# Windowed attention and a gated network on one core: w_out sums moved out of the first pair, a classic second down projection, and activation splits on VectorE

## The chip, the core and the metric

The kernel runs as one program on 1 core of one Trainium2 chip. The metric is the device time of that core in microseconds (us). The core has a matrix engine (TensorE, PE in the profile, with its weight loads as PEld), three engines for elementwise work (VectorE or DVE, ScalarE or ACT, GpSimd or POOL) and SyncE (SP), whose queue starts all the transfers. Each engine works through its own instruction list in order, and waits on semaphores where an operand or a buffer isn't ready.

## The reference

Everything is float32 at the edges; the weights reach the program as 64-bit patterns, which it converts itself. Cut to what matters:

```python
# q, k, v: 8 x 8 x 576 x 64;  w_gate, w_val: 512 x 1536;  w_out: 1536 x 512
scores = 1/sqrt(64) * q @ k^T
scores = where(0 <= i - j < 64, scores, -1e9)        # causal window of 64
attn   = exp(scores - max);  attn = attn / (sum(attn) + 1e-9)
x      = (attn @ v) as 4608 tokens x 512
out    = (sigmoid(x @ w_gate) * (x @ w_val)) @ w_out
```

## The kernel before

**Tiles and pairs.** The 4608 tokens are 12 tiles of 384, worked on as six pairs, which I call pair 0 to pair 5. In each pair a stage of *ups* (x times w_gate and w_val, sigmoid and product: 1536 hidden features for 768 tokens) comes before a stage of *downs* (hidden times w_out). Between these matmuls stand those of the attention that makes x for the next pair. It is cut into eight *units* a pair, each a tile and a quarter of the features. A unit is scores (L219) and softmax minima on VectorE (L243) with exponentials on ScalarE (L251), then the normalization by a factor (L268), on GpSimd but for one quarter, then transposes on TensorE (`pp`, L299) with their copies `pT` on ScalarE (L304), and last the products with v (`oo`, L328), copied out as `xf` by ScalarE (L282, L316).

**Exactness.** A float32 operand is split into a rounded high part and a low rest, and each block product takes three matmuls: high by high, high by low, low by high (`three`, L583). So an activation block needs a *part* before TensorE can use it: a ScalarE copy for the high half (L671), a subtraction for the low half (L673).

**Pair 0** is classic: `up` (L358), sigmoid (L367), gate times value (L386), `down`. Meanwhile the 36 weight blocks (12 each of w_gate, w_val and w_out) arrive as integers and are converted, two ScalarE activations (`conv_a`), three VectorE bit operations (`conv_b`, L126 to L130) and a split (`conv_c`, L158) each. Converted float32 blocks of w_gate and w_val are stored to the scratch arrays `w32d` (L98). As soon as two blocks of w_out are there, `wo_sums` (L462) forms their sums on GpSimd in pieces of 128 columns, and stores them to `wod`.

**Pairs 1 to 5** save matmuls by a Strassen-Winograd scheme: seven block products instead of eight, from four weight sums (S1 to S4) and activation differences (T1 to T4); the table is `PRODUCTS`. The ups of a pair are 84 products of six matmuls (`product`, L612), as six blocks k of seven products n. The downs are 42 parts (seven products of six blocks k), each against two outputs with three matmuls, 252 in all (`last_product`, L676). The differences of x are made by `x_prep` and `x_part` (L562 to L577), those of the hidden blocks by `h_prep` and `h_part` (L661 to L674); `h_engine` and `x_engine` put them on VectorE in pair 1 (but for the last k) and on GpSimd from pair 2 on. `h_part` makes its low half on GpSimd for products 2 and 6. In the ups of pair 1 the gate and value sums are made from `w32d` as well (`sums_load`, `sums_make`, `sums_split`, `sums_store`).

**Order.** TensorE's instructions keep the order of the program. That order comes from due times written by hand: `put(time, order, function, ...)` collects events, the list is sorted, and the functions are called in turn. `visit(("u", i) ...)` and `visit(("d", i) ...)` attach an attention stage of a unit behind up product i or down part i. A scheduler places the instructions of the other engines; a buffer that comes from a pool by its tag (`raw`, `w32`, `W`, `x0` to `x13`, `wo_0` to `wo_6`) makes its new user wait for the last reader of the old one. TensorE's output banks are `b0` and `b1` with three buffers each: ups and downs share them, so a down's first matmul waits for VectorE's last reads of an up's bank (`c` at L625, `h` at L629).

The listing below gives the functions that the change touches, with the lines of the profile.

Of the kernel before, what the change touches and what calls it, by code (L numbers as in the profile page):

```python
# [18 lines left out]
P = 128  # L19
BLK = 64  # L20
TT = 384
# [5 lines left out]
def attn_ffn(ctx: ExitStack, tc: tile.TileContext, qT, kT, vN, w_gate, w_val, w_out, out, outT):  # L27
# [70 lines left out]
    w32d = [[dr.tile([P, DM], F32, name=f"w32d_{m}_{j}") for j in range(NF)] for m in range(2)]  # L98
# [33 lines left out]
    def conv_c(i):  # L132
# [15 lines left out]
        else:  # L148
            cp = split(w32.rearrange("p (a h) -> p a h", a=2), w2[:, :, 0, :], w2[:, :, 1, :], nc.vector)
            wgv[m][j] = w2  # L150
            nc.sync.dma_start(out=w32d[m][J], in_=w32)
            for name, half in (("A11", 0), ("A12", 1)) if J < NK else (("A22", 1),):
                put_part(m, J % NK, name, w2[:, half])
        marks[("w", i)] = (cp,)
# [241 lines left out]
    def get_hidden(t, j):  # L396
        hb = mp.tile([P, 2, TT], F32R, name=f"hb_{t}_{j}", tag="raw", bufs=RAW)
# [63 lines left out]

    def wo_sums(k):  # L462


        cols = [slice(c, c + P) for c in range(0, H, P)]
        b = [xp.tile([P, 3, H], F32, name=f"b{i}_{k}", tag=f"x{12 + i}") for i in range(2)]
        for i in range(2):
            src = wo_all[2 * k + i].bitcast(F32).rearrange("p e (a h) -> p e a h", a=2)
            for a in range(2):
                for c in cols:  # L470
                    nc.gpsimd.tensor_add(out=b[i][:, a, c], in0=src[:, 0, a, c], in1=src[:, 1, a, c])
        for c in cols:
            nc.gpsimd.tensor_add(out=b[0][:, 2, c], in0=b[0][:, 1, c], in1=b[1][:, 1, c])
        for c in cols:
            nc.gpsimd.tensor_sub(out=b[1][:, 2, c], in0=b[0][:, 2, c], in1=b[0][:, 0, c])
        for c in cols:
            nc.gpsimd.tensor_sub(out=b[0][:, 1, c], in0=b[0][:, 0, c], in1=b[0][:, 1, c])
        for c in cols:
            nc.gpsimd.tensor_sub(out=b[1][:, 0, c], in0=b[1][:, 0, c], in1=b[1][:, 2, c])
        for i, (names, at) in enumerate(((("S3", "S1"), (1, 2)), (("S4", "S2"), (0, 2)))):  # L480
            hi = xp.tile([P, 2, H], F32R, name=f"bh{i}_{k}", tag=f"x{10 + i}")
            for e, (name, a) in enumerate(zip(names, at)):
                for c in cols:
                    nc.gpsimd.tensor_copy(out=hi[:, e, c], in_=b[i][:, a, c])
                for c in cols:
                    nc.gpsimd.tensor_sub(out=b[i][:, a, c], in0=b[i][:, a, c], in1=hi[:, e, c].bitcast(F32))
# [461 lines left out]
```

## Time and profile before

| quantity | value |
|---|---|
| median of 3 runs | 1011.53 us |
| lowest and highest | 1008.22 and 1012.38 us |
| the profiled execution, its time | 1010.89 us |
| its span | 1009.1 us |
| mean granted TensorE clock | 0.991 |
| DMA | 275.04 MB, 273 GB/s mean |
| end of pair 0 | 231.6 us from the start of the span |

The span is the time from the first to the last instruction that the profiler saw. The page gives the busy time of each engine, which is an average over stages with different limits: pair 0 has conversions and no Strassen scheme, pair 5 has no attention beside it. So the profile is to be read stage by stage. In a row of groups, "out<-in" gives the operation's result and operands by the names in the program, x the count, and the last part the idle time of the engine ahead of them with the instruction that ended it.

### The profile page before, as it was taken

How to read it: one execution, taken by the hardware profiler on the slowest of the kernel's cores; microseconds unless marked ns; L12 is line 12 of the kernel's file. 1: busy time of each engine (PE TensorE's matmuls, PEld its weight loads, DVE VectorE, ACT ScalarE, POOL GpSimd, SP SyncE). 2: the span in 40 equal slices, each digit the busy share in tenths (PEclk: the TensorE clock that was granted, in tenths of full speed). 3: DMA queues.
4: the chain of work that ended last, by engine and by line, in shares of the span. 5: the costliest groups of instructions: out<-in, count | busy, mean ns of one | idle time of the engine just before them, and what ended most of it. 6: DMA issues, size and time to landing. Idle time of an engine off the chain costs nothing.

```text
span 1009.1 us, 20697 instructions
## 1 busy us (share of the span) xinstructions
PE 956.9 (95%) x7164; PEld 904.2 (90%) x7164; DVE 686.3 (68%) x1681; ACT 588.5 (58%) x1469; POOL 482.3 (48%) x626
## 2 busy tenths in 40 slices
PE   6997998999999899999989999989999989999998
PEld 5886997879998899999889999979999979999988
DVE  7899998856777867555766455776555675655762
ACT  7876776637667565555665555575545666412341
POOL 4269759977673742131755113565122474111552
PEclk9999999999999999999999999999999999999999
DMA  9899998999897689888769888768978865888454
GB/s 347 304 352 337 367 332 293 325 344 328 318 322 257 234 256 313 268 263 263 249 193 307 273 271 262 251 212 280 299 259 263 260 218 190 300 261 248 130 191 164
DMA packets 109832, 275.04 MB, mean 273 GB/s; under 512 B 11936, under 2 KB 42784, under 8 KB 109728
## 3 DMA queue, kind: packets, MB, share of 16 engines
q1 hardware_dynamic: 109728, 273.73, 81.5%
q8 instruction: 57, 0.93, 0.4%
q14 instruction: 47, 0.39, 0.1%
HBM read 220.99 MB, written 52.69 MB: 271 GB/s over the span
## 4 chain that ended last, share of the span: by engine, by line
PE 63%; DVE 18%; ACT 8%; DMA 4%; POOL 3%; issue 3%; SPq 0%; DVEq 0%; POOLq 0%; ACTq 0%
PE pr L586 35%; PE y L586 17%; DVE h L673 7%; PE ph L358 3%; ACT p L251 2%; PE s L219 2%; PE pp L299 2%; PE y L411 2%; DVE h L629 2%; DVE w L130 1%; PE s L328 1%; POOL h L673 1%; DVE w L128 1%; DVE w L158 1%; ACT h L671 1%
## 5 line engine op out<-in xcount | busy, mean ns | idle before, releaser
L586 PE MATMUL y<-h,wot 128*128 128x384 f32 x1260 | 231.0, 341 | 15.3 <-DVE h L673 5.9
L586 PEld LDWEIGHTS y<-h,wot 128*128 128x128 f32 x1260 | 222.1, 191 | 19.8 <-DVE h L673 7.2
L586 PE MATMUL pr<-x_T,wt 128*128 128x384 f32 x1224 | 226.1, 336 | 1.4 <-DVE c L596 1.2
L586 PEld LDWEIGHTS pr<-x_T,wt 128*128 128x128 f32 x1224 | 211.8, 188 | 3.4 <-DVE c L596 2.3
L586 PE MATMUL pr<-x_B,wt 128*128 128x384 f32 x1008 | 187.4, 336 | 0.0
L586 PEld LDWEIGHTS pr<-x_B,wt 128*128 128x128 f32 x1008 | 175.0, 188 | 3.2 <-issue 3.1
L268 POOL TENSOR_TENSOR p<-p,rs 128x384 f32<-128x384 f32 x76 | 68.9, 921 | 207.1 <-DVE rs L259 191.6
L671 ACT CAST h<-h 128x384 fp32r<-128x384 f32 x210 | 100.9, 513 | 79.3 <-PE y L586 39.6
L673 DVE TENSOR_TENSOR h<-h,h 128x384 fp32r<-128x384 f32 x150 | 115.6, 803 | 41.8 <-ACT h L671 41.7
L367 ACT ACTIVATE g<-c 128x384 f32<-128x384 f32 x90 | 47.3, 525 | 141.2 <-DVE c L625 141.0
L251 ACT ACTIVATE p<-p,mn 128x128 f32<-128x128 f32 x288 | 111.1, 393 | 24.6 <-DVE mn L243 24.2
L358 PE MATMUL ph<-x,w 128*128 128x384 f32 x576 | 108.7, 343 | 4.1 <-ACT g L367 2.9
L358 PEld LDWEIGHTS ph<-x,w 128*128 128x128 f32 x576 | 101.5, 191 | 7.2 <-ACT g L367 3.6
L629 DVE TENSOR_TENSOR h<-c,g 128x384 f32<-128x384 f32 x90 | 64.5, 716 | 39.2 <-ACT g L367 33.3
L673 POOL TENSOR_TENSOR h<-h,h 128x384 fp32r<-128x384 f32 x60 | 64.7, 1088 | 53.8 <-ACT h L671 52.9
L243 DVE CUSTOM_DVE_ANT_0 p<-s,m 128x128 f32<-128x128 f32 x288 | 65.4, 283 | 19.8 <-PE s L219 19.8
L596 DVE TENSOR_TENSOR c<-pr,p 128x384 f32<-128x384 f32 x60 | 33.1, 551 | 55.1 <-PE pr L586 55.1
L304 ACT COPY pT<-pp 128x384 f32<-128x384 f32 x96 | 41.3, 480 | 37.7 <-PE pp L299 37.7
L219 PE MATMUL s<-k,q 64*64 64x128 f32 x1152 | 47.5, 292 | 11.6 <-ACT xf L316 5.5
L549 POOL TENSOR_TENSOR h<-h 128x384 f32<-128x384 f32 x21 | 23.7, 1128 | 65.7 <-DVE h L629 65.7
L299 PE MATMUL pp<-ident,p 128*128 128x128 f32 x288 | 43.9, 282 | 9.6 <-POOL p L268 6.8
L219 PEld LDWEIGHTS s<-k,q 64*64 64x64 f32 x1152 | 34.4, 140 | 18.6 <-ACT xf L316 6.4
(114 smaller groups left out, 1500.5 us busy)
## 6 DMA issues: line engine op xcount, KB each, us to landing
wt<-wd SPq DMA_DIRECT2D x186, 512.0 KB, 4.4
wot<-wod SPq DMA_DIRECT2D x105, 512.0 KB, 4.4
v<-in_vN_dram SPq DMA_DIRECT2D x48, 384.0 KB, 5.2
wd<-ws SPq DMA_DIRECT2D x48, 256.0 KB, 5.3
k<-in_kT_dram SPq DMA_DIRECT2D x48, 224.0 KB, 4.8
q<-in_qT_dram SPq DMA_DIRECT2D x48, 192.0 KB, 4.6
wd<-w SPq DMA_DIRECT2D x36, 256.0 KB, 5.1
out_dram<-yo SPq DMA_DIRECT2D x39, 192.0 KB, 4.6
```

Of the source, the lines that this page charges most:

```text
L219: pe(nc.tensor.matmul(sc[h][half * BLK:(half + 1) * BLK, u, :], qt[h * BLK:(h + 1) * BLK, U * BLK:(U + 1) * BLK], kt[h * BLK:(h + 1) * BLK ...
L243: nc.vector.tensor_tensor_reduce(out=pt[:, u, :], in0=sc[:, u, :], in1=masks[key], op0=ALU.add, op1=ALU.min, scale=-SCALE, scalar=3.0e38, ...
L251: exp = nc.scalar.activation(pt[:, u, :], pt[:, u, :], AF.Exp, bias=mn[:, u:u + 1], scale=-1.0, **sums)
L268: eng.tensor_mul(out=pt, in0=pt, in1=rs.unsqueeze(2).broadcast_to([P, UP, P]))
L299: pe(nc.tensor.transpose(pp[:, u, :], pt[:, u, :], ident))
L304: cp = nc.scalar.copy(pT, pp)
L358: pe(nc.tensor.matmul(ph, l, r, start=i == 0, stop=i == len(prs) - 1))
L367: act = nc.scalar.activation(g, c, AF.Sigmoid)
L586: pe(nc.tensor.matmul(ps, l, r, start=first and i == 0, stop=last and i == 2, skip_group_check=not check))
L629: nc.vector.tensor_mul(out=hidden(s, k)[2 * r + b], in0=c, in1=gates.pop((t, j)))
L671: nc.scalar.copy(h2[:, 0, :], src)
L673: eng.tensor_sub(out=h2[:, 1, :], in0=src, in1=h2[:, 0, :].bitcast(F32))
```

## The change

It has six edits.

- **No w_out sums in pair 0.** `wo_sums` becomes `wo_sums_load` and a new `wo_sums`, on VectorE (seven operations) and ScalarE (three copies), from blocks stored in `w32d`, which now holds w_out too (12 more stores of 256 KB). Each of the six sums is a round: two loads, the sums, eight stores of 128 KB to `wod`. They are due 11 us apart, from part 24 of pair 1's downs (counted in steps of half a part) on, and the last end in the ups of pair 2.
- **Classic downs in pair 1.** `plain_part` and `plain_down` replace the seven products there: two tiles times twelve hidden blocks are 24 parts, each against four output blocks, 288 matmuls. They use w_out as converted; positions 10 and 11 are stored away at the end of pair 0 (`keep_wo`) and fetched again (`fetch_wo`). `hidden` takes other buffers for pair 1, and `h_prep` isn't called there. `get_hidden` takes buffers of the x tags for j over 5.
- **All activation work on VectorE.** `x_engine` and `h_engine` go; the differences and both kinds of splits are on VectorE in every pair, and `h_split` is the common helper.
- **Splits begun within the ups.** The first twelve `h_part` of a pair are due from 12.4 us ahead of its downs; the loads of w_out blocks (`wo_load`) have new due times.
- **Seven units within the ups.** From pair 2 on, unit 0 of the next pair has its scores behind up product 0, instead of at down part 34 of the pair before, its normalization behind product 1 and its transposes behind product 3. Unit 6's transposes move from down part 4 to part 8.
- **Times.** The first two blocks of the gate and value sums and `wo_parts` (the stores of plain w_out blocks) move within pair 1.

```diff
-    w32d = [[dr.tile(... name=f"w32d_{m}_{j}") for j in range(NF)] for m in range(2)]
+    w32d = [[dr.tile(... name=f"w32d_{m}_{j}") for j in range(NF)] for m in range(3)]
...
     def get_hidden(t, j):
-        hb = mp.tile([P, 2, TT], F32R, name=f"hb_{t}_{j}", tag="raw", bufs=RAW)
+        if j > 5:
+            hb = xp.tile([P, 2, TT], F32R, name=f"hb_{t}_{j}", tag=f"x{10 + (j + 2) % 4}")
+        else:
+            hb = mp.tile([P, 2, TT], F32R, name=f"hb_{t}_{j}", tag="raw", bufs=RAW)
...
+    def wo_sums_load(k):
+        a = mp.tile([P, 2, DM], F32, name=f"wa_{k}", tag="raw", bufs=RAW)
+        for i in range(2):
+            nc.sync.dma_start(out=a[:, i, :], in_=w32d[2][k + i * NK])
...
     def wo_sums(k):
+        nc.vector.tensor_add(out=s1, in0=a[:, 0, 1, :], in1=a[:, 1, 1, :])
+        nc.vector.tensor_sub(out=s2, in0=s1, in1=a[:, 0, 0, :])
+        nc.scalar.copy(b[:, 2:4, :].bitcast(F32R), b[:, 0:2, :])
+        nc.vector.tensor_sub(out=s3, in0=a[:, 0, 0, :], in1=a[:, 0, 1, :])
+        nc.vector.tensor_sub(out=s4, in0=a[:, 1, 0, :], in1=s2)
+        nc.scalar.copy(c[:, 0, :].bitcast(F32R), s3)
+        nc.scalar.copy(c[:, 1, :].bitcast(F32R), s4)
+        nc.vector.tensor_sub(out=b[:, 0:2, :], in0=b[:, 0:2, :], in1=b[:, 2:4, :])
...
+    def h_split(nm, i, src):
+        h2 = xp.tile([P, 2, TT], F32R, name=f"h_{nm}", tag=f"x{i % (2 * NPR)}")
+        nc.scalar.copy(h2[:, 0, :], src)
+        nc.vector.tensor_sub(out=h2[:, 1, :], in0=src, in1=h2[:, 0, :].bitcast(F32))
+        return h2
...
+    PLAIN = [(k, r) for k in (1, 2, 3, 4, 5, 0) for r in range(2)]
...
+            three(ps, wo_all[2 * k + r], d, hs[i], x == 0, x == NF - 1)
...
-        if m == 2 and j % 2:
-            put(tm + 5, 7.2, wo_sums, j // 2)
...
+            if s > 1:
+                visit(("u", 0), 3, *unit(s + 1, 0))
+                visit(("u", 1), 4, *unit(s + 1, 0))
+            visit(("u", 3 if s > 1 else 1), 1, *unit(s + 1, 0))
             for v in range(1, NP * 2 - 1):
                 visit(("u", NPR * v - 2), 3, *unit(s + 1, v), unit(s + 1, v - 1), spare_up)
+                visit(("u", NPR * v - 1), 4, *unit(s + 1, v))
+                visit(("u", NPR * v + 2) if v < 6 else ("d", 8), 1, *unit(s + 1, v))
...
-        if s + 2 < NS:
-            visit(("d", 34), 3, *unit(s + 2, 0))
-            visit(("d", 36), 4, *unit(s + 2, 0))
...
+            for k in range(NK):
+                put(at_down[24] + 4 + 11 * k, 7, wo_sums_load, k)
+                put(at_down[24] + 12 + 11 * k, 7, wo_sums, k)
...
         for i, tm in enumerate(at_down):
-            put(t0 + i - 8 + (tm - t0 - PRT * i) if i > 7 else t0 + i - 8, 5.2, h_part, s, *divmod(i, NK))
+            if i < 12:
+                when = max(t0 - 14.5 + 2.1 * (i // 2 + 1), {5: t0 - 3.9, 11: t0 + 0.8}.get(i, t0 - 20))
+            else:
+                when = at_down[i - 14] + 1.2 if i > 13 else t0 + 1
+            put(when, 5.2, h_part, s, *divmod(i, NK))
```

Three places show what moves. In the rows a name's last figure is only a running number; an "x" at the end counts equal neighbours.

The first is GpSimd's list in pair 0, before the change, at the first `wo_sums` (`b` and `bh` are its buffers, `w` the converted blocks of w_out, `p` a softmax tile with its factors `rs`).

```order
L471 TENSOR_TENSOR b_0_1089<-w_0_937 128x128 x4
L471 TENSOR_TENSOR b_0_1090<-w_1_1025 128x128 x4
L473 TENSOR_TENSOR b_0_1089<-b_0_1089,b_0_1090 128x128 x2
L268 TENSOR_TENSOR p_2_0_1042<-p_2_0_1042,rs_0_1044 128x384
L475 TENSOR_TENSOR b_0_1090<-b_0_1089 128x128
L477 TENSOR_TENSOR b_0_1089<-b_0_1089 128x128
L484 CAST bh_0_1107<-b_0_1089 128x128
```

And the same stretch of GpSimd's list after it:

```order
L268 TENSOR_TENSOR p_1_3_739<-p_1_3_739,rs_3_729 128x384
L268 TENSOR_TENSOR p_2_0_1058<-p_2_0_1058,rs_0_1060 128x384
L268 TENSOR_TENSOR p_2_0_1070<-p_2_0_1070,rs_0_1060 128x384
L268 TENSOR_TENSOR p_2_2_1340<-p_2_2_1340,rs_2_1342 128x384
L268 TENSOR_TENSOR p_2_2_1352<-p_2_2_1352,rs_2_1342 128x384
```

The 40 instructions of each sum, which stood between the softmax factors, are gone, and only the factors remain.

The second is TensorE's list at the start of pair 2's downs, before the change (`y` are the two outputs in work, `h_2_0` to `h_2_5` the parts of one product by block k, `wot` the loaded w_out blocks, `pp_7_1` the transposes of an attention unit of tile 7).

```order
L586 MATMUL y_0_2_6824<-h_2_3_6724,wot_1_6579 128x384 x3
L586 MATMUL y_1_2_6828<-h_2_3_6724,wot_1_6579 128x384 x3
L586 MATMUL y_0_2_6824<-h_2_4_6736,wot_2_6605 128x384 x3
L586 MATMUL y_1_2_6828<-h_2_4_6736,wot_2_6605 128x384 x3
L299 MATMUL pp_7_1_6880<-ident,p_7_1_6768 128x128 x3
L299 MATMUL pp_7_1_6886<-ident,p_7_1_6778 128x128 x3
L586 MATMUL y_0_2_6824<-h_2_5_6786,wot_2_6605 128x384 x3
```

And after it (the line of the matmuls is now L597):

```order
L597 MATMUL y_0_2_6643<-h_2_5_6566,wot_2_5780 128x384 x3
L597 MATMUL y_1_2_6647<-h_2_5_6566,wot_2_5780 128x384 x3
L597 MATMUL y_0_2_6722<-h_2_0_6532,wot_3_5893 128x384 x3
L597 MATMUL y_1_2_6726<-h_2_0_6532,wot_3_5893 128x384 x3
L597 MATMUL y_0_2_6722<-h_2_1_6536,wot_3_5893 128x384 x3
L597 MATMUL y_1_2_6726<-h_2_1_6536,wot_3_5893 128x384 x3
L597 MATMUL y_0_2_6722<-h_2_2_6559,wot_4_6009 128x384 x3
L597 MATMUL y_1_2_6726<-h_2_2_6559,wot_4_6009 128x384 x3
L299 MATMUL pp_7_1_6755<-ident,p_7_1_6598 128x128 x3
L299 MATMUL pp_7_1_6761<-ident,p_7_1_6608 128x128 x3
```

The transposes stood behind the fifth part of the first product; now they stand behind the whole first product and three parts of the second.

The third is VectorE's list in pair 1's downs, just ahead of the softmax minima of the last attention unit (`p_5_3` with `mn`, their minima), before the change:

```order
L673 TENSOR_TENSOR h_1_5_4949<-h_1_5_4739,h_1_5_4949 128x384
L673 TENSOR_TENSOR h_1_4_5115<-h_1_4_4521,h_1_4_5115 128x384
L673 TENSOR_TENSOR h_1_5_5126<-h_1_5_4739,h_1_5_5126 128x384
L673 TENSOR_TENSOR h_1_0_5135<-h_0_3495,h_1_0_5135 128x384
L243 ISA p_5_3_5051,mn_5_3_5052<-s_5_3_5021,m_81 128x128
```

And after it (`h_p` are parts of the classic downs, `wa`, `wb` and `wc` the buffers of a w_out sum, here the second):

```order
L705 TENSOR_TENSOR h_p_4708<-h_1_2_3760,h_p_4708 128x384
L478 TENSOR_TENSOR wb_5137<-wa_5070 128x256
L479 TENSOR_TENSOR wb_5137<-wb_5137,wa_5070 128x256
L481 TENSOR_TENSOR wa_5070<-wa_5070 128x256
L482 TENSOR_TENSOR wa_5070<-wa_5070,wb_5137 128x256
L485 TENSOR_TENSOR wb_5137<-wb_5137 128x512
L486 TENSOR_TENSOR wa_5070<-wa_5070,wc_5138 128x256
L705 TENSOR_TENSOR h_p_4729<-h_1_3_4018,h_p_4729 128x384
L487 TENSOR_TENSOR wa_5070<-wa_5070,wc_5138 128x256
L243 ISA p_5_3_4768,mn_5_3_4769<-s_5_3_4738,m_81 128x128
```

The seven VectorE operations of a sum, which need the loaded blocks and ScalarE's copies, now stand in the queue ahead of the minima.

More of the change, by code (lines that the diff above doesn't have):

```diff
@@ L97, in attn_ffn @@
     KINDS = 3
-    w32d = [[dr.tile([P, DM], F32, name=f"w32d_{m}_{j}") for j in range(NF)] for m in range(2)]
+    w32d = [[dr.tile([P, DM], F32, name=f"w32d_{m}_{j}") for j in range(NF)] for m in range(3)]
     H = DM // 2
@@ L460, in wo_parts @@
                                   in_=wo_all[pos][:, :, half * H:(half + 1) * H].bitcast(F32))
-    def wo_sums(k):
[L465 to L486, printed above, removed]
-                nc.sync.dma_start(out=wo_at(k, name)[:, 0, :], in_=hi[:, e, :].bitcast(F32))
-                nc.sync.dma_start(out=wo_at(k, name)[:, 1, :], in_=b[i][:, a, :])
@@ L820, in attn_ffn @@
             put(now - 19 + 10 * c + 1.2 * n, 5.6, x_rest, 1, n, c)
-    for k in range(NK):
-        put(now - 24 + 2 * k, 8.6, wo_parts, k)
+    for x, pos in enumerate(KEPT):
+        put(now - 14 + 4 * x, 8.6, keep_wo, pos)
     for s in range(1, NS):
```

128 lines of the change are left out of this document (97 added, 31 removed).

## The prediction

> **What bounds the kernel now.** I read the engine shares first, then the busy times of the stretches between the ends of the stages, then the matrix engine's rows in order of time at the places where a stretch shows idle.
>
> ```profile
> PE 956.9 (95%) x7164; PEld 904.2 (90%) x7164; DVE 686.3 (68%) x1681; ACT 588.5 (58%) x1469; POOL 482.3 (48%) x626
> 50.00:231.60 181.60, 166.81 (x1177) 147.77 (x1176) 156.10 (x356) 120.13 (x275) 144.26 (x235) 0.98 0.97 337
> 231.60:339.40 107.80, 105.50 (x829) 98.94 (x827) 80.05 (x193) 69.55 (x169) 66.44 (x124) 1.00 0.87 295
> 339.40:392.70 53.30, 49.90 (x361) 47.75 (x361) 37.92 (x93) 37.04 (x100) 28.16 (x26) 1.00 0.84 269
> 392.70:496.60 103.90, 103.44 (x830) 99.36 (x828) 62.42 (x163) 56.18 (x144) 30.71 (x31) 1.00 0.83 267
> 496.60:552.60 56.00, 51.43 (x360) 49.29 (x361) 37.13 (x89) 37.53 (x100) 31.91 (x30) 0.97 0.76 242
> 656.50:711.00 54.50, 49.89 (x361) 47.73 (x361) 37.58 (x89) 37.33 (x100) 32.29 (x30) 1.00 0.77 248
> 814.90:869.90 55.00, 50.44 (x338) 48.72 (x338) 35.70 (x76) 35.63 (x88) 29.82 (x28) 0.97 0.69 223
> 869.90:957.20 87.30, 87.30 (x505) 87.30 (x504) 51.58 (x91) 24.15 (x47) 19.96 (x18) 1.00 0.71 227
> ```
>
> The rows are pair 0 without its start, then ups and downs of pair 1, of pair 2, the downs of pairs 3 and 4, and the ups of pair 5. The columns are the length, the busy time of PE, PEld, DVE, ACT and POOL, the granted clock, the DMA share and GB/s. The last row is the undisturbed rate: 505 matmuls in 87.30 us, 0.173 us each, with PE never idle. So PE is the bound nearly everywhere, and only two things can shorten the program: fewer matmuls, or less of PE's idle time, which sits in two kinds of place. In pair 0 PE lacks 14.8 us (181.60 less 166.81) while VectorE is busy for 86%. In every downs stretch of pairs 1 to 4 it lacks 3.4 to 4.6 us, but only 0.5 us in the ups of pair 2. The downs lose it at their start, which pair 3 shows:
>
> ```profile
> 657.50 5.48 PE L586 MATMUL y<-h,wot 128*128 128x384 f32 x30 [0.99 <-ACT xf L282]
> 663.76 0.55 PE L299 MATMUL pp<-ident,p 128*128 128x128 f32 x3 [0.78 <-POOL p L268]
> 664.55 0.55 PE L299 MATMUL pp<-ident,p 128*128 128x128 f32 x3 [0.24 <-POOL p L268]
> 674.44 0.44 PE L586 MATMUL y<-h,wot 128*128 128x384 f32 x1 [1.42 <-ACT h L671]
> 676.06 8.44 PE L586 MATMUL y<-h,wot 128*128 128x384 f32 x47 [1.18 <-DVE h L673]
> 970.01 0.44 PE L586 MATMUL y<-h,wot 128*128 128x384 f32 x1 [1.18 <-ACT h L671]
> 971.63 33.66 PE L586 MATMUL y<-h,wot 128*128 128x384 f32 x185 [1.18 <-DVE h L673]
> ```
>
> Start and length come first; the bracket is the wait ahead. The first four stops of pair 3 are the late copy of an attention output, the late softmax factor (twice), and the late activation part; the last two rows are pair 5, which has no attention and stops for the part alone.
>
> **The change part by part.** *Pair 0 without the w_out sums.* GpSimd's list loses 240 instructions there. Three of their groups, with the VectorE rows that run beside them:
>
> ```profile
> L471 POOL TENSOR_TENSOR b<-w 128x128 f32<-128x128 f32 x48 | 31.0, 677 | 26.4 <-issue 13.2 <-PE ph L358 8.1 <-DVE mn L243 2.2
> L486 POOL TENSOR_TENSOR b<-b,bh 128x128 f32<-128x128 f32 x48 | 30.2, 647 | 0.0
> L484 POOL CAST bh<-b 128x128 fp32r<-128x128 f32 x48 | 22.3, 478 | 0.0
> L126 DVE TENSOR_SCALAR zz<-w x36: 412/551/1047, 15.4 to 184.3; 128x512 int32<-128x512 int32 x36
> L128 DVE SCALAR_TENSOR_TENSOR w<-w,zz x36: 677/824/1315, 16.4 to 185.1; 128x512 int32<-128x512 int32 x36
> L130 DVE CUSTOM_DVE_ANT_0 w<-raw,w x36: 678/806/983, 17.2 to 185.9; 128x1024 uint16<-128x1024 uint16 x36
> L158 DVE TENSOR_TENSOR w<-w,w x36: 654/692/1312, 19.8 to 188.0; 128x512 fp32r<-128x512 f32 x36
> ```
>
> At least 83.5 us of GpSimd work go. The four VectorE steps of a weight conversion have medians 0.139, 0.147, 0.128 and 0.038 us above their shortest (the figures are shortest/median/longest in ns); I lay that 0.45 us to GpSimd, and 36 conversions give 16 us, which takes VectorE from 156 to about 140 of 181.6. The waits of PE that this feeds:
>
> ```profile
> 69.70 0.55 PE L299 MATMUL pp<-ident,p 128*128 128x128 f32 x3 [1.81 <-POOL p L268]
> 77.16 0.88 PE L219 MATMUL s<-k,q 64*64 64x128 f32 x22 [1.51 <-ACT xf L316]
> 88.13 2.38 PE L358 MATMUL ph<-x,w 128*128 128x384 f32 x12 [1.54 <-ACT g L367]
> 100.37 1.31 PE L219 MATMUL s<-k,q 64*64 64x128 f32 x22 [3.15 <-ACT xf L316]
> 168.02 2.38 PE L358 MATMUL ph<-x,w 128*128 128x384 f32 x12 [1.12 <-DVE h L386]
> 171.80 2.35 PE L358 MATMUL ph<-x,w 128*128 128x384 f32 x12 [1.40 <-ACT g L367]
> 178.97 1.29 PE L328 MATMUL oo<-pT,v 128*64 128x64 f32 x14 [2.08 <-ACT pT L304]
> ```
>
> They make 12.6 us. One waits for GpSimd outright, the others for ScalarE or VectorE, whose queues are in order behind the conversions. I take two thirds, **-8.4** (ends 0 and -12.6). The 12 new stores of converted w_out (256 KB) stand against 48 removed ones of 128 KB, so the transfers of pair 0 fall.
>
> *Half clock.* Right behind three of these stops, and of those above, PE runs at half rate:
>
> ```profile
> 100.67:104.08 3.41, 3.41 (x30) 3.08 (x22) 3.11 (x15) 3.38 (x10) 3.41 (x8) 0.50 1.05 395
> 517.10:520.51 3.41, 3.41 (x12) 3.41 (x12) 2.70 (x14) 3.08 (x15) 1.48 (x3) 0.50 0.43 159
> 676.10:679.50 3.40, 3.40 (x20) 3.40 (x21) 2.72 (x16) 3.12 (x14) 2.27 (x2) 1.00 0.59 206
> 971.07:974.48 3.41, 2.85 (x9) 2.85 (x10) 3.41 (x7) 0.64 (x2) 1.25 (x1) 0.50 0.03 13
> ```
>
> 12 matmuls instead of 20 cost 1.4 us. I find five such stretches (at 100.67, 179.18, 517.10, 834.53 and 971.07) and let three go with the stops: **-4.2** (ends 0 and -7). The Trainium skill, "TensorE: Matmul & The Clock Gate", section "HAM oscillation — how this bites in real kernels", wants only idle gaps over about 3.4 us avoided; by it these short stops would cost no clock and this term would be 0. The trace differs: the row at 971.07 stands behind two gaps of 1.18 us.
>
> *Pair 1, ups.* They take 107.8 where pair 2 takes 103.9. VectorE loses the 12 differences of the sums of activations that a classic down doesn't want, and GpSimd keeps the weight sums: **-2** (ends 0 and -3.9).
>
> *Pair 1, classic downs.* 24 activation parts against four output blocks with three matmuls each are 288 matmuls; seven products of six parts, two outputs and three matmuls were 252. The 36 more cost 36 x 0.173 = **+6.2**, all of it on PE. The 3.4 us of idle in the old stretch go (**-3.4**): the parts are made ahead. In their place stands a new wait. The six w_out sums now run on VectorE and ScalarE inside these downs, each behind a load, and the second of them stands ahead of the softmax minima of the last attention unit. The transfers of this size:
>
> ```profile
> a<-w32d SPq DMA_DIRECT2D x16, 256.0 KB, 5.3
> wod<-b SPq DMA_DIRECT2D x12, 128.0 KB, 3.2
> wd<-ws SPq DMA_DIRECT2D x6, 256.0 KB, 7.0
> ```
>
> The second load may only start when the first sum's stores have landed (its buffer). I count from the start of the downs: first sum done at 9 us, stores landed by 10, load landed 3.5 to 5.3 later, seven VectorE steps of at most 0.56, then minima to factor as now in 5.2 us. That gives 23 to 26 for a transpose that PE reaches at 23. I take **+2.5** with the first unit's own late factor (ends 0 and +5).
>
> *Pairs 2 to 4.* All activation parts are now on VectorE and begin 14.5 us before the downs, and the first transposes stand behind nine parts instead of five, 4.2 us later. VectorE's price for a part:
>
> ```profile
> L673 DVE TENSOR_TENSOR h<-h,h x150: 543/559/1410, 326.9 to 985.1; 128x384 fp32r<-128x384 f32 x150
> L673 POOL TENSOR_TENSOR h<-h,h x60: 1000/1017/1396, 345.8 to 991.4; 128x384 fp32r<-128x384 f32 x60
> L268 POOL TENSOR_TENSOR p<-p,rs x76: 825/830/1343, 7.8 to 839.4; 128x384 f32<-128x384 f32 x76
> ```
>
> GpSimd gave about 36 operations a pair at 1.0 us or more; VectorE takes them at 0.56, 20 us, into pairs of 160 us where it is busy for 62 + 37. That fits, and the part that was late (the second product's of the last k) no longer passes three GpSimd steps. But the steps that free PE's banks now queue behind some 20 more VectorE operations, so I keep 1.6 us of each pair's 5.1 (0.5 in the ups, 4.6 in the downs): 3 x -3.5 = **-10.5** (ends 0 and -15.3). Every stop also drains the array (one matmul of 0.44 at 674.44 where 0.17 is the rate); four stops fewer a pair make 3 x -1 = **-3**. Pair 5 loses its two stops, **-2.4** (ends 0 and -2.4).
>
> *Seven units within the ups.* The next pair's first scores move from the end of the downs to behind the first product, so their matmuls are moved, not added. Their transposes come three products later, 6.2 us, where the steady units have four: softmax may be late by some tenths, 3 x 0.5 = **+1.5** (ends 0 and +4).
>
> The sum: -8.4 - 4.2 - 2 + 6.2 - 3.4 + 2.5 - 10.5 - 3 - 2.4 + 1.5 = -23.7. The profiled execution took 1010.89 (its span 1009.1), which gives 987.2; the median of the runs is 0.6 above it, so **987.8**.
>
> **The rivals.** *The waits move instead of going.* VectorE reaches the bank-freeing steps of each last k late, behind its new work, and PE stops there. For it: those stretches already end on VectorE and ScalarE rows. Against: its 0.56 us price. Half of the terms of pairs 2 to 5 come back (8), and half of pair 0's (4): 1000.
>
> *Slower: the chain of w_out rounds.* Each sum waits for its load, the next load for stores, and pair 2's first activation parts stand behind the fourth and fifth sum on VectorE. The second load lands at about 14, the last four rounds later; pair 2 needs its parts near 60 after the downs' start. A round of 9 us (load 5, sum 4) has slack; from (60 - 14)/4 = 11.5 us each further microsecond costs 4. With loads and stores that both need 7.0, as the busiest row above shows, and the sum between, a round is 18 and PE loses 4 x 6.5 = 26: 1014; at 19 us it is 1018, slower than before. Against it: these downs no longer load their 21 blocks of 512 KB.
>
> *The change does little:* pair 0's waits are ScalarE's own (its share there is 66%) and stay, and the classic down's 36 matmuls eat what the transitions give: 987.8 + 8.4 + 4.2 + 8 = 1008.4.
>
> *No clock returned:* as worked out from the rows, without the half-clock term, 992.
>
> *GpSimd blocked:* the softmax factors stay there, 0.83 us alone and up to 1.34 beside others; two of them ahead of each transition's transposes cost 1.0 a pair, 3 in all: 990.8. The Trainium skill, "SBUF — State Buffer", section "Who interferes with whom", says that a VectorE instruction with two inputs in SBUF and a GpSimd instruction that reads SBUF lock each other out, which speaks against more such work on VectorE; the two longest times above agree.
>
> **How the numbers follow.** Forecast (978 to 997) 0.40, no clock returned 0.08, GpSimd blocked 0.07, more than forecast (below 978, most terms at their good ends) 0.10, waits move 0.17, does little 0.08, slower chain 0.10. A measurement of this kernel tells about 0.5% from no change, so faster means below 1006.5: 0.82; within 0.08; slower 0.10. The range reaches from 972 (pair 0 and the transitions nearly clean: 4.2 + 4.8 + 2.8 + 1.9 + 2.5 below the sum) to 1005, where the moved waits end.
>
> **What would show it.** Right: PE idle in pair 0's stretch falls from 14.8 to about 6; the downs of pairs 2 to 4 take some 50 us with stops under 1 us; pair 1's downs take 57 to 59. Wrong: PE rows that wait for VectorE's c or h just ahead of the downs, a stop of several microseconds at the second transposes of pair 1's downs or at pair 2's first products, or waits in pair 0 that look as before although GpSimd idles.

## The result, and the profile after

The changed kernel takes **980.97 us** (median of 4 runs, 977.43 to 981.22) against 1011.95 (median of 4, 1008.22 to 1014.05), a ratio of 0.969 with a 95% interval of 0.9653 to 0.9726. The prediction was 987.8 in a range of 972 to 1005. The profiled execution took 980.85, its span is 979.0, 30.1 less than before.

First the engine shares of the page and its row of activation parts (busy time, mean ns), then the busy times of the stages, with the columns of the prediction: pair 0 without its start, ups and downs of pair 1, of pair 2, the downs of pairs 3 and 4, and those of pair 5.

```profile
PE 953.7 (97%) x7200; PEld 906.8 (93%) x7200; DVE 697.2 (71%) x1873; ACT 589.0 (60%) x1473; POOL 142.7 (15%) x232
...
L705 DVE TENSOR_TENSOR h<-h,h 128x384 fp32r<-128x384 f32 x168 | 93.3, 584 | 17.9 <-ACT h L704 17.7
```

```profile
50.00:212.20 162.20, 160.78 (x1177) 144.79 (x1176) 136.15 (x356) 121.25 (x278) 31.77 (x44) 1.00 0.95 348
212.20:318.40 106.20, 104.51 (x829) 99.41 (x828) 72.41 (x191) 69.38 (x173) 52.91 (x112) 1.00 0.87 293
318.40:372.70 54.30, 54.30 (x374) 53.43 (x373) 33.62 (x98) 28.44 (x78) 0.00 (x0) 1.00 0.76 254
372.70:484.80 112.10, 108.02 (x854) 102.85 (x854) 72.93 (x206) 63.30 (x170) 9.69 (x12) 0.97 0.84 276
484.80:534.10 49.30, 48.64 (x338) 47.20 (x337) 39.54 (x97) 34.48 (x86) 4.17 (x4) 1.00 0.85 272
...
639.60:688.90 49.30, 48.66 (x338) 47.22 (x338) 39.56 (x97) 34.51 (x86) 4.17 (x4) 1.00 0.86 273
...
794.40:843.70 49.30, 48.65 (x338) 47.20 (x337) 39.57 (x97) 34.49 (x86) 4.17 (x4) 1.00 0.77 245
...
931.00:975.20 44.20, 43.89 (x253) 43.52 (x252) 26.88 (x55) 18.21 (x37) 0.00 (x0) 1.00 0.61 198
```

The first two columns of a row give TensorE's idle time, and that is what went: 1.4 us are left of 14.8 in pair 0, none of 3.4 in pair 1's downs, and 0.7 of 4.6 in the downs of each of pairs 2 to 4. The stage that became longer by far the most is the ups of pair 2. By stage, before and after:

| stage | before | after | change | forecast for it |
|---|---|---|---|---|
| pair 0 | 231.6 | 212.2 | -19.4 | -8.4, and up to two half-clock stretches of 1.4 |
| pair 1 ups, downs | 107.8, 53.3 | 106.2, 54.3 | -1.6, +1.0 | -2, +5.3 |
| pair 2 ups, downs | 103.9, 56.0 | 112.1, 49.3 | +8.2, -6.7 | about -4 in all, less clock |
| pair 3 ups, downs | 103.9, 54.5 | 105.5, 49.3 | +1.6, -5.2 | about -4 in all |
| pair 4 ups, downs | 103.9, 55.0 | 105.5, 49.3 | +1.6, -5.7 | about -4 in all, less clock |
| pair 5 downs | 48.1 | 44.2 | -3.9 | -2.4, less clock |

The start of pair 3's downs, TensorE's rows in order of time, answers to the five stops that the prediction showed there. One of 0.56 is left:

```profile
639.58 9.53 PE L597 MATMUL y<-h,wot 128*128 128x384 f32 x54
648.95 0.55 PE L299 MATMUL pp<-ident,p 128*128 128x128 f32 x3
650.05 0.55 PE L299 MATMUL pp<-ident,p 128*128 128x128 f32 x3 [0.56 <-POOL p L268]
```

### The profile page after: what moved, and what is told of

Same layout as the page of the kernel before. It is cut to its first block, busy times and chain, and to the rows that moved or that the text cites. A ratio compares the mean times of both kernels' runs of the same rounds, so it can differ in the third digit from the quotient of the medians.

```text
span 979.0 us, 20624 instructions
## 1 busy us (share of the span) xinstructions
PE 953.7 (97%) x7200; PEld 906.8 (93%) x7200; DVE 697.2 (71%) x1873; ACT 589.0 (60%) x1473; POOL 142.7 (15%) x232
## 4 chain that ended last, share of the span: by engine, by line
PE 67%; DVE 12%; ACT 7%; DMA 5%; issue 3%; POOL 3%; SPq 1%; DVEq 0%; POOLq 0%; ACTq 0%
PE pr L597 31%; PE y L597 14%; PE ph L358 10%; PE y L414 5%; PE s L219 3%; ACT p L251 2%; DVE h L705 2%; DMA a<-w32d 2%; PE pp L299 2%; DMA wa<-w32d 2%; PE s L328 1%; POOL ws L550 1%; DVE h L571 1%; PE oo L328 1%; DVE h L640 1%
## 5 line engine op out<-in xcount | busy, mean ns | idle before, releaser
L597 PE MATMUL pr<-x_T,wt 128*128 128x384 f32 x1224 | 226.5, 336 | 4.4 <-DVE c L607 3.6
L597 PEld LDWEIGHTS pr<-x_T,wt 128*128 128x128 f32 x1224 | 211.8, 188 | 8.0 <-DVE c L607 5.9
L597 PE MATMUL pr<-x_B,wt 128*128 128x384 f32 x1008 | 189.6, 339 | 0.0
L597 PEld LDWEIGHTS pr<-x_B,wt 128*128 128x128 f32 x1008 | 176.8, 190 | 3.3 <-issue 2.9
L597 PE MATMUL y<-h,wot 128*128 128x384 f32 x1008 | 178.9, 336 | 0.3 <-DVE h L640 0.3
L597 PEld LDWEIGHTS y<-h,wot 128*128 128x128 f32 x1008 | 174.4, 188 | 1.4 <-DVE h L640 0.6
L704 ACT CAST h<-h 128x384 fp32r<-128x384 f32 x168 | 81.8, 513 | 52.1 <-PE y L597 30.8
L358 PE MATMUL ph<-x,w 128*128 128x384 f32 x576 | 106.1, 338 | 0.0
L705 DVE TENSOR_TENSOR h<-h,h 128x384 fp32r<-128x384 f32 x168 | 93.3, 584 | 17.9 <-ACT h L704 17.7
L640 DVE TENSOR_TENSOR h<-c,g 128x384 f32<-128x384 f32 x90 | 54.9, 610 | 46.1 <-ACT g L367 40.7
L607 DVE TENSOR_TENSOR c<-pr,p 128x384 f32<-128x384 f32 x60 | 33.1, 552 | 40.1 <-PE pr L597 40.1
L251 ACT ACTIVATION_READ_ACCUMULATOR p<-p,mn 128x1 f32 x264 | 49.7, 188 | 0.0
L636 DVE TENSOR_TENSOR c<-pr,p 128x384 f32<-128x384 f32 x60 | 33.1, 555 | 20.3 <-PE pr L597 20.2
## 6 DMA issues: line engine op xcount, KB each, us to landing
k<-in_kT_dram SPq DMA_DIRECT2D x48, 224.0 KB, 5.0
```

What stands on the lines that cost most here:

```text
L251: exp = nc.scalar.activation(pt[:, u, :], pt[:, u, :], AF.Exp, bias=mn[:, u:u + 1], scale=-1.0, **sums)
L358: pe(nc.tensor.matmul(ph, l, r, start=i == 0, stop=i == len(prs) - 1))
L597: pe(nc.tensor.matmul(ps, l, r, start=first and i == 0, stop=last and i == 2, skip_group_check=not check))
L640: nc.vector.tensor_mul(out=hidden(s, k)[2 * r + b], in0=c, in1=gates.pop((t, j)))
L704: nc.scalar.copy(h2[:, 0, :], src)
L705: nc.vector.tensor_sub(out=h2[:, 1, :], in0=src, in1=h2[:, 0, :].bitcast(F32))
```

## The experiments

**What made pair 0 shorter?** In the kernel before, I replaced the sums by the plain halves, stored at the same place:

```diff
     def wo_sums(k):
-        ... 40 adds, subtractions and casts on GpSimd
+        for name, i, half in (("S3", 0, 0), ("S1", 0, 1), ("S4", 1, 0), ("S2", 1, 1)):
+            src = wo_all[2 * k + i].bitcast(F32)
+            for e in range(2):
+                nc.sync.dma_start(out=wo_at(k, name)[:, e, :], in_=src[:, e, half * H:(half + 1) * H])
```

> The kernel before, but pair 0 stores the halves of w_out as they are in place of their sums: GpSimd's 240 operations are left out (so the products S1 to S4 of the downs use wrong weights), the 48 stores of 128 KB stay, and so does all the rest. Theory (GpSimd's sums slowed pair 0): pair 0 ends at 211 to 214 us instead of 231.6, and the program takes about 992 to 994. Rival (the saved stores, the free buffers or the other hidden-block buffers bring a part of it): pair 0 ends at 217 to 226, the program takes 997 to 1006. The forecast's own size (8.4 and about 2.8 of half clock) would be an end at 220.

It took 1002.58 (median of 4; ratio 0.9893, 0.9863 to 0.9923), and pair 0 ended at 224.0. Its window, and the conversion steps on VectorE (shortest, median and longest ns):

```profile
50.00:223.90 173.90, 163.94 (x1176) 146.25 (x1175) 135.41 (x360) 121.32 (x279) 30.24 (x46) 0.99 1.02 359
```

```profile
L126 DVE TENSOR_SCALAR zz<-w x36: 391/423/920, 15.4 to 182.8; 128x512 int32<-128x512 int32 x36
```

```profile
L128 DVE SCALAR_TENSOR_TENSOR w<-w,zz x36: 677/686/1318, 16.4 to 183.5; 128x512 int32<-128x512 int32 x36
```

```profile
L130 DVE CUSTOM_DVE_ANT_0 w<-raw,w x36: 676/689/1202, 17.2 to 185.4; 128x1024 uint16<-128x1024 uint16 x36
```

The medians fall from 0.551, 0.824 and 0.806 to 0.423, 0.686 and 0.689, and VectorE's busy time from 156.1 to 135.4. So GpSimd did slow VectorE as the prediction said; but leaving its work out gives only 7.6 of the 19.4 us, and 1.7 of them are clock (one half-clock stretch in this pair 0, two before). The rival took the rest. The DMA share is 1.02 here, 0.95 in the changed kernel. ScalarE's rows ahead of a TensorE stop of 3.02 us at 76.62 show one thing that waits:

```profile
75.03 0.66 ACT L117 ACTIVATE w<-raw 128x512 f32<-128x512 f32 x1 [1.03 <-DMA w32d<-w]
75.59 0.60 ACT L157 CAST w<-w 128x512 fp32r<-128x512 f32 x1
76.10 0.47 ACT L316 COPY xf<-oo 128x384 f32<-128x384 f32 x1
```

A conversion waits until its buffer has been stored; the copy `xf`, which TensorE needs, stands behind it in ScalarE's queue. This wait is 1.03 of the 3.02 us. So next I queued the 48 stores in pair 1's ups, behind a k load:

```diff
+                with tc.issue_after(marks["k"]):
                     nc.sync.dma_start(out=wo_at(k, name)[:, e, :], in_=src[:, e, half * H:(half + 1) * H])
...
-            put(tm + 5, 7.2, wo_sums, j // 2)
+        put(now + 6 + 8 * k, 8.6, wo_sums, k)
```

> As the run with the unsummed halves of w_out (GpSimd's sums left out, so S1 to S4 are wrong), but the 48 stores of 128 KB are queued in the ups of pair 1 instead of in pair 0. In the earlier run pair 0 ended at 224.0 us, 7.6 less than before and 11.8 more than in the changed kernel. Theory (the stores in SyncE's queue and their traffic hold up the weight loads, and these the conversions): pair 0 ends at 212 to 215 us. Rival (the rest comes from the hidden blocks' buffers or from another order): pair 0 still ends at 220 to 224.

Pair 0 ended at 216.3, 7.7 earlier. The program took 1031.74, because the stores now held up the queue in pair 1 (TensorE stopped for 22.6 and 11.2 us there); only pair 0 is read. The windows of its first 100 us:

```profile
0.00:50.00 50.00, 39.90 (x500) 33.82 (x501) 38.80 (x176) 40.18 (x121) 16.44 (x28) 0.97 0.88 321
50.00:100.00 50.00, 48.21 (x350) 44.26 (x349) 46.83 (x124) 42.11 (x92) 4.13 (x4) 0.97 1.02 367
```

A clock of 0.97 over 50 us is a stretch of about 3.4 us at half speed, 1.7 us lost, twice. The changed kernel has none in pair 0, so most of the last 4.1 us is clock; what the hidden blocks' other buffers bring wasn't tried alone. Without the clock, GpSimd's work is worth 5.9 us and the moved stores 9.4, each by a single profile (the first run's is of the slowest of its four executions, 1004.97).

By which wait the stores cost this stays open. ScalarE's waits for stores of conversion buffers didn't fall from one run to the other (1.9 us between 50 and 190, then 3.3); what fell is its wait for VectorE's last bit step (L130), from 24.4 us to 9.7. Nor were the stores all that moved: ScalarE's and VectorE's instructions in pair 0 came out in another order (as they had when GpSimd's work was left out), and seven loads of w_out blocks (512 KB each), which wait for these stores, left the end of pair 0 with them. So "another order", which the rival named, isn't excluded.

The other direction: the changed kernel with the old GpSimd work back, its results unused.

```diff
+        if m == 2 and j % 2:
+            put(tm + 5, 7.2, pool_sums, j // 2)    # the old wo_sums without its stores
```

> The changed kernel with the old 240 operations on GpSimd added back in pair 0, their results used by nobody and stored nowhere; correct output. Theory: pair 0 ends again at 228 to 232 us instead of 212.2, the program takes 996 to 1001. Rival (what counted were the stores and the buffers, which do not come back here): pair 0 ends below 220, the program takes less than 989.

It took 1006.78, and pair 0 ended at 239.8, later than in the kernel before:

```profile
50.00:239.70 189.70, 168.84 (x1182) 150.05 (x1181) 157.68 (x361) 123.69 (x281) 144.72 (x236) 0.96 0.87 297
```

VectorE is back at 157.7, and the clock fell to 0.96. The direction is that of the theory, the size isn't: 27.6 us here, 7.6 in the other surrounding. Part of the difference took a way that neither theory named. Behind the added work GpSimd is late with the weight sums of pair 1's ups (`sw`); ScalarE waits for them, and TensorE's longest stop, 5.35 us up to 206.16, follows:

```profile
202.32 0.51 ACT L614 CAST x_B<-xf 128x384 fp32r<-128x384 f32 x1 [4.17 <-POOL sw L560]
```

The clock is at half from 203.9 to 214.1, so this place alone costs some 9 us. In the kernel before, ScalarE waits for `sw` only once in pair 0, for 1.75 us at its end. So this run shows that GpSimd's work makes pair 0 longer, and not by how much it did so before.

> As the run with the old operations back on GpSimd, but the softmax factors of tiles 0 to 3 (28 on GpSimd at 0.83 us) are on VectorE (0.56 each, some 15 us more there). Theory A (GpSimd's work slows VectorE's own instructions, and the queues behind those are late): pair 0 still ends at 226 us or later, with the conversion steps as long as before. Theory B (the factors stood behind the sums in GpSimd's queue): pair 0 ends at 213 to 218.

```diff
-        eng = nc.vector if t == 3 and p % 2 or t // 2 == 2 else nc.gpsimd
+        eng = nc.vector if t < 6 else nc.gpsimd
```

With the factors on VectorE pair 0 ended at 238.9 (1006.15). That is later than 226, as theory A has it, but the conversion steps weren't as long as before (medians 0.428, 0.693 and 0.740). The stops at transposes that waited for GpSimd's factor (2.17, 2.49 and 2.33 us in the run before) went, others at ScalarE's copies grew. Theory B alone is out; but VectorE got some 15 us of new work with it, so this doesn't weigh theory A by itself.

**What removed the stops of the downs: the engine or the early start?**

```diff
-            if i < 12: when = max(t0 - 14.5 + 2.1 * (i // 2 + 1), ...)
-            else: when = ...
+            when = t0 + i - 8 + (tm - t0 - PRT * i) if i > 7 else t0 + i - 8
```

> The changed kernel with the activation parts of pairs 2 to 5 due as before, from 8 us ahead of the downs instead of 12.4, in the old spacing; all on VectorE still. Theory A (the early start removed the stops of the downs): downs of pairs 3 and 4 take 51 to 54 us instead of 49.3, ups 104.7 instead of 105.5; program slower by 3 to 12. Theory B (VectorE's price of 0.56 us was enough): downs stay at 49.3 to 50, and the ups lose the stop of about 1 us at their last products; program faster by 1 to 3.

The instructions of all five engines came out in the very order of the changed kernel: the due times of these parts didn't decide their places. So neither theory was tested, and the early due times do nothing. The parts begin no earlier than in the kernel before, either: VectorE's first split for pair 3 stands 14.5 us ahead of its downs there (642.96 against 657.50), and 13.7 in the changed kernel (625.91 against 639.58). But the run is a second execution of the same order: 977.41. Pairs 3 and 4 agree to 0.02 us. Pair 2's ups took 108.8 instead of 112.1 (below).

> The changed kernel with the differences of x and h and the splits of products 2 and 6 of pairs 2 to 5 back on GpSimd (1.0 us each), at the new, early times. Theory A (early times are what counted): downs of pairs 3 and 4 stay at 49.3 to 50.5 us; program within 4 of 981. Theory B (GpSimd's price and its softmax factors made the parts and transposes late): downs take 51 to 55, program 989 or more.

```diff
-            src = rhs_of(nc.vector, ...)                      # and differences(nc.vector, ...)
+            src = rhs_of(nc.gpsimd, ...)                      # pairs 2 to 5, x and h
+            eng = nc.gpsimd if n in (2, 6) else nc.vector     # the split's subtraction
```

It took 995.85, 15 to 18 more, and the downs of pairs 3 and 4 took 54.0, as before the change. TensorE's rows at pair 3:

```profile
640.73 9.64 PE L597 MATMUL y<-h,wot 128*128 128x384 f32 x54 [0.99 <-ACT xf L282]
...
654.28 1.00 PE L328 MATMUL s<-pT,v 128*64 128x64 f32 x15 [1.16 <-ACT pT L304]
...
657.63 0.45 PE L597 MATMUL y<-h,wot 128*128 128x384 f32 x1 [1.24 <-ACT h L704]
659.25 3.23 PE L597 MATMUL y<-h,wot 128*128 128x384 f32 x11 [1.17 <-DVE h L705]
```

The last two stops are those of the kernel before (1.42 and 1.18) at the same place. Theory B holds: the engine made the difference. And GpSimd costs more than its own 1.0 us a part: beside its steps, three of VectorE's splits took 3.98 us in this run (as at 645.66 in the kernel before), and 1.49 in the changed kernel:

```profile
628.88 3.98 DVE L705 TENSOR_TENSOR h<-h,h 128x384 fp32r<-128x384 f32 x3
```

```profile
629.18 1.49 DVE L705 TENSOR_TENSOR h<-h,h 128x384 fp32r<-128x384 f32 x3
```

> The changed kernel with the first attention unit of pairs 3 to 5 back at the end of the downs (scores at part 34, transposes behind the ups' second product). Forecast's term: the new place costs 0.5 us a pair through late softmax, so ups of pair 3 take 104.2 us (0.8 of scores moved, 0.5 of wait), downs 50.1, program faster by 1 to 2. Rival: no wait stands there; ups 104.7, downs 50.1, program within 1 of 981, except pair 2's start, where the late sums may cost as much or less.

```diff
-                visit(("u", 0), 3, *unit(s + 1, 0))
-                visit(("u", 1), 4, *unit(s + 1, 0))
-            visit(("u", 3 if s > 1 else 1), 1, *unit(s + 1, 0))
+            visit(("u", 1), 1, *unit(s + 1, 0))
...
+            visit(("d", 34), 3, *unit(s + 2, 0))
+            visit(("d", 36), 4, *unit(s + 2, 0))
```

Pair 3 took 104.47 and 50.32, in all 154.79; the changed kernel's 105.51 and 49.28 make the same sum. The place of the first unit costs nothing in the steady pairs. The program took 978.52; most of the 2.3 us that it lies under the changed kernel's profile are in pair 1's ups (104.4 instead of 106.2), which the edit doesn't touch.

**What stops pair 2's ups?** TensorE's rows at their start, of the changed kernel and then of the second execution of its order:

```profile
388.95 1.00 PE L328 MATMUL s<-pT,v 128*64 128x64 f32 x15 [1.25 <-ACT pT L304]
...
391.72 1.56 PE L219 MATMUL s<-k,q 64*64 64x128 f32 x24 [1.47 <-DMA k<-in_kT_dram]
393.20 4.21 PE L597 MATMUL pr<-x_B,wt 128*128 128x384 f32 x12
```

```profile
387.66 1.00 PE L328 MATMUL s<-pT,v 128*64 128x64 f32 x15 [0.71 <-ACT pT L304]
...
390.96 0.89 PE L219 MATMUL s<-k,q 64*64 64x128 f32 x24 [2.01 <-DMA k<-in_kT_dram]
391.78 4.43 PE L597 MATMUL pr<-x_B,wt 128*128 128x384 f32 x24
```

The stops make 2.72 us in both. But in the first, 12 matmuls behind them take 4.21 us, in the second 24 take 4.43: half clock. The changed kernel's ScalarE and SyncE rows show where the stops come from:

```profile
386.71 1.28 ACT L367 ACT_TABLE_LOAD   x1 [5.99 <-DMA out_dram<-yo]
```

```profile
368.69 0.45 SPq L468 DMA_DIRECT2D wa<-w32d  x1
369.23 0.40 SPq L446 DMA_DIRECT2D wot<-wod  x1
373.71 0.32 SPq L490 DMA_DIRECT2D wod<-wb  x1
...
379.26 0.32 SPq L491 DMA_DIRECT2D wod<-wa  x1
...
380.65 3.29 SPq L731 DMA_DIRECT2D out_dram<-yo  x4
...
386.71 0.42 SPq L180 DMA_DIRECT2D k<-in_kT_dram  x1
```

SyncE stands from 369.6 to 373.7 at the first store of the sixth sum, whose second load was issued only at 368.69. Behind its stores are the four output stores of pair 1, which free the buffers that the first sigmoid wants (they share a tag), and behind those q and k. ScalarE's queue stands at that sigmoid for 6 us, with the copies `pT` behind it. To test this, the last two rounds went behind a k load of pair 2:

```diff
+            with tc.issue_after(marks["k"]) if k > 3 else nullcontext():
                 nc.sync.dma_start(out=a[:, i, :], in_=w32d[2][k + i * NK])
```

> The changed kernel with the loads of the last two of the six w_out sums queued behind a k load of the ups of pair 2, so behind the output stores of pair 1. Theory (the stores of the last sums hold up the queue: the output stores behind them free the buffer of the first sigmoid late, and q and k land late): the ups of pair 2 take 105.5 to 106.5 us instead of 112.05, with no stop at their first scores, and the program takes 974 to 976. Rival (the stop has another cause, such as ScalarE's copies or the position of the units): the ups stay above 109, the program at 979 or more. Risk: the later sums make the w_out blocks of pair 2's downs late, which would show as a stop there.

One execution took 976.65; pair 2's ups took 108.7, not 105.5 to 106.5. The two stops went, and two others came (0.73 behind a sigmoid, 1.51 at VectorE's u, where the moved sums now are). The result lies between the ranges of theory and rival.

> The same kernel as in the look with the last two w_out sums behind a k load of pair 2's ups, now timed. Its one execution took 976.65, but an execution with the changed kernel's own instruction order took 977.41, with pair 2's ups at 108.77 instead of 112.05. Theory (moving two rounds helps): median 975 to 977.5, ratio 0.964 to 0.967, pair 2's ups below 109 each time. Rival (it only traded one stop for another): median 977.5 to 981, as the changed kernel.

Five executions have a median of **976.68** (975.33 to 977.86; ratio 0.9652, 0.9631 to 0.9674), with pair 2's ups at 107.6 in the one that was profiled. That is the best version here, 4.3 under the changed kernel's median, though the intervals of the two ratios overlap, and some of it isn't the edit's: pair 1's ups, ahead of the moved rounds, took 104.3 in this profile and 106.2 in the changed kernel's. Moving all six rounds should have done more:

```diff
-                put(at_down[24] + 4 + 11 * k, 7, wo_sums_load, k)
-                put(at_down[24] + 12 + 11 * k, 7, wo_sums, k)
+                put(now + 6 + 11 * k, 7, wo_sums_load, k)     # behind a k load
+                put(now + 14 + 11 * k, 7, wo_sums, k)         # behind VectorE's newest combination
```

> The changed kernel with all six w_out sums moved out of pair 1's downs into the ups of pair 2: each round's loads stand behind a k load in SyncE's queue, its first VectorE steps behind the last combination; the w_out loads that need the sums are 25 us later. Theory (the rounds at the end of the downs make the stops at pair 2's start, 3 to 6 us with a spread from run to run): pair 2's ups take 105.5 to 107 us (112.05 and 108.77 in two executions of the changed kernel's order), and the program takes 974 to 976. Rival (the stops belong to the transition itself, which is the first with q and k loads of a steady pair): ups stay at 108 or more. Third: the rounds stop TensorE somewhere within the ups, which would show as a wait for VectorE's u or c in the middle.

It took 986.05, pair 2's ups 117.4. The third possibility came true: TensorE stopped within the ups for VectorE, twice for 2 us, while VectorE's rows show it without a gap, a sum's steps between the minima and the hidden products:

```profile
450.79 1.69 PE L600 MATMUL pr<-x_B,wt 128*128 128x384 f32 x6 [2.13 <-DVE h L643]
...
471.73 2.04 PE L600 MATMUL pr<-x_B,wt 128*128 128x384 f32 x6 [1.96 <-DVE h L643]
```

```profile
447.07 0.42 DVE L481 TENSOR_TENSOR wb<-wb,wa 128x256 f32<-128x256 f32 x1
447.41 0.42 DVE L484 TENSOR_TENSOR wa<-wa 128x256 f32<-128x256 f32 x1
447.75 0.55 DVE L639 TENSOR_TENSOR c<-pr,u 128x384 f32<-128x384 f32 x1
448.43 0.56 DVE L567 TENSOR_TENSOR xf<-xf,xf 128x384 f32<-128x384 f32 x1
448.91 0.42 DVE L485 TENSOR_TENSOR wa<-wa,wb 128x256 f32<-128x256 f32 x1
...
450.18 0.55 DVE L643 TENSOR_TENSOR h<-pr,g 128x384 f32<-128x384 f32 x1
```

The place in pair 1's downs, where VectorE is busy for 33.6 of 54.3 us, is the better one for most rounds.

**The last 1.5 us of the steady pairs.** Each keeps 1.0 us of stops at its last products (VectorE's u and c) and 0.56 at the transposes. Two experiments, the first on top of the six moved rounds, the second on top of the two:

```diff
     def h_part(s, n, k, held):
+        with tc.issue_after(marks["v"]) if held else nullcontext():     # newest combination
             hs[(s, n, k)] = h_split(...)
```

> As the run with the rounds in the ups of pair 2, and besides, the softmax factors of the last two attention units of pairs 3 to 5 on VectorE, and the first twelve activation parts of each pair queued behind the newest combination on VectorE. Theory: the stop of 0.55 us at the transposes (waits for GpSimd's factor) goes, and of the 1.0 us of stops at the last products of the ups most go too: ups of pairs 3 and 4 take 104.6 to 105 us instead of 105.5, downs 48.8 instead of 49.3; the program 970 to 973. Rival (VectorE is full in those 15 us, 625 to 640 in the profile, so whatever is put first there makes the next late): the downs get a stop for activation parts of about 1 us each instead, and the program stays within 1.5 of the run without it.

> As the kernel with the two late rounds, and the first twelve activation parts of each pair 2 to 5 queued behind the newest combination on VectorE, at the changed kernel's due times, factors on GpSimd. Theory (the combinations were late only because parts were put ahead of them): ups of pairs 3 and 4 take 103.7 to 104.2 us instead of 105.5, downs at most 0.5 more than 49.3; program 971 to 974. Rival (VectorE is full there; parts put later make the reciprocal of the softmax later, and the transposes wait for the factor): downs 50.5 to 52.5, program 975 to 982.

The first took 993.91, the second 981.43 (median of 4; ratio 0.9698, 0.9678 to 0.9719). In both the ups of pairs 3 and 4 fell to 103.7, and the downs rose, to 53.4 and 52.7. TensorE's row at pair 3's transposes, first with the factor on VectorE, then on GpSimd:

```profile
656.32 0.99 PE L299 MATMUL pp<-ident,p 128*128 128x128 f32 x6 [3.56 <-DVE p L268]
```

```profile
643.92 0.55 PE L299 MATMUL pp<-ident,p 128*128 128x128 f32 x3 [2.27 <-POOL p L268]
```

The rival's way is right, though the downs grew by more than either rival said (4.1 and 3.5 us), and the first program by 7.9 over the run that it builds on: VectorE is full there, and what is put off delays the softmax reciprocal. It stands 8.0 us behind the start of pair 3's downs in the changed kernel, 11.4 in the first of these runs and 10.4 in the second.

## Why the prediction was right, and where it was not

- **The mechanism** was right: fewer matmuls weren't the gain (36 were added), TensorE's idle time was. Pair 0 and the downs lost it.
- **"I take two thirds, -8.4"** for pair 0 was the term that was mis-sized most. Nearly all its stops went: idle 14.8 became 1.4, and TensorE's busy time fell by 6.0 as well (166.81 to 160.78; two half-clock stretches are 3.4 of it). The step that failed is "the transfers of pair 0 fall", to which I gave no price; with the stores queued later, pair 0 ended 7.7 us earlier, as much as the 7.6 of GpSimd's work, though that run changed the order of other work too. I had laid the late conversions to GpSimd alone.
- **The half clock**, -4.2: before had five stretches, and all five went, worth 1.7 us each rather than 1.4. A new one of 6.8 us (390.8 to 397.6) came in pair 2, which takes back up to 3.4. How many there are changes with the execution: the mean clocks of the changed kernel's four are 0.996, 0.992, 0.998 and 0.998.
- **Classic downs**, +6.2 - 3.4 + 2.5: measured +1.0. The +2.5 failed. I had the first sum done 9 us into the downs; its load was issued 5.4 us ahead of them, at 313.0, and it was done at 7.7. The second load didn't wait until the first sum's stores had landed: it was issued at 326.67, 0.2 us behind the last of them. The second sum ended 15.3 us into the downs, the softmax factors 21.0, and the transposes came at 22.3 without a wait. That leaves 1.8 below 6.2 - 3.4, which I put down to the scores that left this stage (1.0 by the run with the unit put back) and to slow restarts; the classic downs weren't tried alone.
- **Pairs 3 to 5**: forecast about -4 a pair and -2.4; measured -3.6, -4.1 and -3.9, the last two each with a half-clock stretch of 1.7 gone, so -2.4 and -2.2 without it. The price of 0.56 us a part was right (0.584 on the page). The cause "begin 14.5 us before the downs" was not: they began as early before the change, and the due times change no order. The engine did it. What I kept back for the bank-freeing steps, 1.6 us a pair, is the size of what is left there: 1.0 at the last products, and 0.56 at the transposes, which is the rival's wait for GpSimd's factor.
- **Seven units within the ups**, +1.5: nothing, as the run with the unit put back showed. The ups' +1.6 is 1.0 of moved scores and 0.5 more of stops, at the last products.
- **Pair 2**: forecast about -4, measured +1.5 in this profile and -1.8 in the second execution. This is the rival of the rounds, at another place: not the activation parts were late, but the output stores and q and k behind the sixth sum in SyncE's queue. It cost 2.7 us of stops, and up to 3.4 of half clock where that followed.

The sum of the forecast, -23.7, met -30.1 because the surplus of pair 0 (8) and of pair 1's downs (4) outweighed pair 2 (5.5). That these errors partly cancel is luck.

## What to carry to other kernels

When an engine's wait ends with another engine's copy, follow that engine's queue back until it ends at a transfer or a buffer; in pair 2 that led from TensorE's wait for `pT` over a sigmoid and its buffer to a store of a sum in SyncE's queue. In pair 0 it wasn't done ahead of the forecast, and taking 48 stores away brought 7.7 us, though no TensorE row named a store. Side work on an in-order queue must be placed where its input has landed: a store that waits for a sum holds up the loads behind it. Before you credit a change of due times, compare the order of the instructions: here it was the same.

## What was not expected of the hardware

Half clock follows the same stops at one place and not at another. In the kernel before, the downs of pairs 3 and 4 have the same two stops, of 1.42 and 1.18 us. Behind pair 3's the clock stayed at 1.00 (the prediction's row at 676.10); behind pair 4's it was 0.50:

```profile
832.80 0.44 PE L586 MATMUL y<-h,wot 128*128 128x384 f32 x1 [1.42 <-ACT h L671]
834.42 5.82 PE L586 MATMUL y<-h,wot 128*128 128x384 f32 x23 [1.18 <-DVE h L673]
```

```profile
834.54:837.95 3.41, 3.41 (x11) 3.41 (x12) 2.73 (x16) 3.12 (x15) 2.17 (x2) 0.50 0.19 48
```

In pair 2 of the changed kernel, stops of 1.25 and 1.47 us came with the window below; in the second execution of the same order, stops of 0.71 and 2.01 us were followed by a clock of 1.00.

```profile
390.80:397.60 6.80, 5.88 (x38) 5.55 (x39) 3.02 (x16) 4.86 (x18) 0.00 (x0) 0.50 1.02 415
```

So a stop of this size has a price with a chance in it, 1.7 us a stretch and up to 3.4 here, which no sum of waits shows. The Trainium skill, "TensorE: Matmul & The Clock Gate", section "HAM oscillation — how this bites in real kernels", speaks of gaps over about 3.4 us; no single gap at these places is that long, so by these runs shorter ones in a row are enough at times, and so was a single one of 2.08 us (ahead of 178.97 in the kernel before, with half clock from 179.18).

The conversion medians fell from 0.824 to 0.686 and from 0.806 to 0.689 once GpSimd idled. The Trainium skill, "SBUF — State Buffer", section "Who interferes with whom", has VectorE instructions with two inputs in SBUF lock out GpSimd's reads and the other way; these medians agree.
